# Attention scores in four 64x64 quarters of the array, two units at a time; probabilities times values in float32 without splits; the preceding block's values loaded from HBM

## The chip, the core and the metric

The program runs on one core of one Trainium2 chip. The metric is the device time of one execution in microseconds (us). Before the change the median of three runs is 838.9 us (837.33 to 839.96).

In the profile PE is TensorE multiplying, PEld is TensorE loading its stationary operand, DVE is VectorE, ACT is ScalarE, POOL is GpSimd, and SP is the engine that issues most transfers. L498 is line 498 of the kernel.

## The reference: what is computed

Attention with a window and a few global keys, then a mixture of experts:

```python
# q, k, v: [4 sequences, 8 heads, 768 tokens, 64]; n_global = 8, n_local = 96
scores = q @ k^T / 8 + bias[h, distance]          # bias: -slope(h) * distance
scores = where(global or 0 <= distance < n_local, scores, -1e9)
a = softmax(scores)
x = concat_heads(a @ v)                           # 3072 tokens x 512
logits = x @ w_gate + log1p(exp(x @ w_noise)) * noise
top 2 of 8 experts for each token, softmax over the two
out = sum over the two of  w * (relu(x @ w1[e]) @ w2[e])     # 512 -> 1024 -> 512
```

Everything is float32 in and out.

## The kernel before

The 3072 tokens are 24 blocks of 128, six to a sequence. A block of queries needs only its own 128 keys, the last 96 of the block before, and the 8 global keys. The 64 queries of one half of a block need 168 columns of keys in all (a window, `WIN`); in the first block of a sequence it is the block's own 128 columns.

**Units.** A unit is one block and one pair of heads; 24 blocks by 4 pairs make 96 units, and 16 of them belong to the first blocks of sequences. `score(n)` (from L488) makes the scores of unit n: for each half of the queries one float32 matmul, L498, with the queries of both heads as stationary operand. The query buffer holds the two heads of a pair on the two halves of the partitions, with zeros opposite (`clear`, L405), so that the contraction runs over all 128 rows and each head meets only its own keys. DVE then adds the bias and takes the extreme (L501), and ACT takes the exponential (L505). `trans(n)` (L510) turns the probabilities by TensorE (L519) and ACT writes them to SBUF as float16 (L521). `rest(n)` (L524) has DVE write what float16 lost, as a second float16 tile (L528). `attend(n)` (L533) multiplies by the values, L553: for each head and each of the two blocks of keys five 16-bit products, of two parts of the probabilities with three bfloat16 parts of the values. Each value row ends in a column of ones per head, so that the 65th output column is the softmax's denominator; every second unit DVE divides (L558 to L561).

**Values.** `load_v` brings a block's values from HBM. POOL splits them into the three parts (`split_v`, L356 and L357). `prev_v` copies the last 96 rows of the split tile to a tile of its own, from SBUF to SBUF (L363), and `keep_globals` does the same for the global keys' rows (L367).

**Order.** The program's order of instructions is the order written; no scheduler moves anything. In step n of the attention loop stand trans(n), score(n+2), rest(n), attend(n-2), and then what is due at that step: loads, the block's gate (`gate_t` L185, `gate_l` L193, `gate_s` L199), clearing of the output, weight loads and weight splits. Steps of the routing (`route`) are spread between as small DVE operations. `gate_l` runs in four 128x32 quarters of the array (a `tile_position` per matmul). SP issues transfers strictly in order and waits where a buffer is not free.

**Experts.** After the attention come eight experts, each with two matrices that are split into two float32r parts; their products (L737, L770, L780) fill TensorE. Expert 0's rows are gathered by table (`gather`, L147) and turned (`turn`, L164) at the attention's end.

**PSUM.** The eight banks are given out by tag: two for scores, two for turned probabilities, two for the products with values, one for the gate's temporaries, one for logits.

Of the kernel before, what the change touches and what calls it, by code (L numbers as in the profile page):

```python
# [10 lines left out]
F32 = mybir.dt.float32  # L11
FR = mybir.dt.float32r
F16 = mybir.dt.float16
# [17 lines left out]
def tile_local_global_attention_then_moe(  # L31
    ctx: ExitStack,
    tc: tile.TileContext,
    q: bass.AP,        # [B, 2, 2, D, S/128, H/2, 64]: halves of a sequence, then even and odd heads
    kT: bass.AP,       # [B, H*D, NB*(NG+P)]: each block of keys behind a copy of the first NG keys
    v: bass.AP,        # [B, NB, P, H*(D+1)]: a column of ones behind each head
    w_gn: bass.AP,     # [Dm, 2*E]: w_gate beside w_noise
    noise: bass.AP,    # [P, NT*E]
    w1: bass.AP,       # [E, Dm, F]
    w2: bass.AP,       # [E, F, Dm]  # L40
    n_global: int,
    n_local: int,
    out: bass.AP,      # [DUMP + N, Dm]
# [18 lines left out]
    SEG = [(0, 6), (6, 12), (12, 17), (17, 21), (21, NT)]   # blocks of tokens that are routed together  # L62
    CLOSE = 2        # after this part the first tiles of expert 0 are closed
# [11 lines left out]
    def bank(tag, bufs):  # L75
        return psum.tile([P, 512], F32, name=tag, tag=tag, bufs=bufs)
# [26 lines left out]
    # raw weights come in halves, in the order of their use  # L103
# [19 lines left out]
    def split(e, x, j, eng=nc.vector):  # L123
        """Piece j of 8 of a matrix into a part that the tensor engine takes as it is and the rest."""
# [29 lines left out]
    def spare_bank():  # L154
        spare[0] += 1
        return bank("m" if spare[0] % 2 else "lg", 1)
# [12 lines left out]
    NZ = 8      # pieces of the result that are cleared beside the attention  # L169
# [5 lines left out]
    # ---------------------------------------------------------------- gate  # L175
    XR, XT, LS = {}, {}, {}
    lg = bank("lg", 1)
    lgv = lg[:, :NT * 2 * E].rearrange("p (t e) -> p t e", t=NT)

    def gate_t(g):  # L180
        x = XR.pop(g).rearrange("p h d -> p (h d)")
        nc.sync.dma_start(xd[DUMP + g * P:DUMP + (g + 1) * P], x)
        ps = bank("m", 1).rearrange("p (k t) -> p k t", k=KC)
# [5 lines left out]
    def gate_l(g):  # L189
        ps = bank("m", 1)[:, :P]  # L190
# [13 lines left out]
    def route(r):  # L204
        """Routes a segment; a generator, to be resumed between steps of what runs beside it."""
# [97 lines left out]
        if r == CLOSE:  # L303
            # the first tiles of expert 0 are closed here: their products run while the rest is routed
# [10 lines left out]
    # ---------------------------------------------------------------- attention  # L315
    with ExitStack() as actx:
# [8 lines left out]
        def load_qk(b, j, i0):  # L325
            """Queries and keys of a block."""
# [615 lines left out]
```

## Time and profile before

| | |
|---|---|
| median of three runs | 838.9 us |
| span of the profiled execution, first to last instruction | 831.3 us |
| first matmul | 5.4 us after the span's start |
| attention, up to expert 0's first product | about 214 us |
| experts | about 617 us |
| PE busy over the span | 792.8 us, 95% |
| DVE, ACT, POOL busy | 379.5, 340.9, 278.4 us |
| mean granted clock of TensorE | 0.987 |

The profile does not record the profiled execution's own time, only its span; the median lies 7.6 us above that. Busy time on PE counts a matmul from its start until its modelled end, so a busy PE can still hold room between starts. How closely matmuls follow each other is read from the starts in the timeline. A float32 product appears as two rows for each instruction (L498: 192 instructions, 384 rows), a transpose as one.

### The profile page before, as it was taken

How to read it: one execution, taken by the hardware profiler on the slowest of the kernel's cores; microseconds unless marked ns; L12 is line 12 of the kernel's file. 1: busy time of each engine (PE TensorE's matmuls, PEld its weight loads, DVE VectorE, ACT ScalarE, POOL GpSimd, SP SyncE). 2: the span in 40 equal slices, each digit the busy share in tenths (PEclk: the TensorE clock that was granted, in tenths of full speed). 3: DMA queues.
4: the chain of work that ended last, by engine and by line, in shares of the span. 5: the costliest groups of instructions: out<-in, count | busy, mean ns of one | idle time of the engine just before them, and what ended most of it. 6: DMA issues, size and time to landing. Idle time of an engine off the chain costs nothing. (4 is left out here: it accounts for less than half of the span.)

```text
span 831.3 us, 16339 instructions
## 1 busy us (share of the span) xinstructions
PE 792.8 (95%) x6321; PEld 708.4 (85%) x6321; DVE 379.5 (46%) x1212; ACT 340.9 (41%) x736; POOL 278.4 (33%) x267
## 2 busy tenths in 40 slices
PE   5998999989898999999999999999999999999994
PEld 5987899878687989898989889898988889898983
DVE  7877889999640444233323332341333234233300
ACT  4766777666341343223323323332333333223311
POOL 8324565576455231314031321403141221212023
PEclk9998999999999999999999999999999999999998
DMA  8899979896456243435344534424344433432014
GB/s 193 229 302 260 261 204 265 222 223 160 175 103 123 66 130 113 96 76 142 102 62 122 131 76 97 118 75 109 114 92 114 105 80 116 96 77 30 1 25 61
DMA packets 86546, 106.93 MB, mean 129 GB/s; under 512 B 35563, under 2 KB 48107, under 8 KB 86459
## 3 DMA queue, kind: packets, MB, share of 16 engines
q1 hardware_dynamic: 71194, 79.10, 34.0%
q0 software_dynamic: 15264, 26.69, 17.4%
q8 instruction: 52, 0.85, 0.4%
q14 instruction: 36, 0.29, 0.1%
HBM read 67.20 MB, written 28.24 MB: 115 GB/s over the span
## 5 line engine op out<-in xcount | busy, mean ns | idle before, releaser
L755 POOL DMA_INDIRECT out_dram<-y,tba x28 | 44.4, 1587 | 257.7 <-ACT y L754 257.7
L132 DVE TENSOR_TENSOR w1l<-raw,w1h 128x512 fp32r<-128x512 f32 x56 | 38.3, 690 | 148.0 <-ACT w1h L131 148.0
L770 PE MATMUL av<-w2h,hh 128*128 128x512 f32 x256 | 102.8, 401 | 0.0
L770 PE MATMUL av<-w2h,hl 128*128 128x512 f32 x256 | 101.3, 396 | 0.0
L770 PE MATMUL av<-w2l,hh 128*128 128x512 f32 x256 | 101.1, 395 | 0.0
L505 ACT ACTIVATE a<-ns,mx 128x168 f32<-128x168 f32 (+1 forms) x192 | 72.6, 423 | 54.7 <-DVE mx L501 46.9
L737 PE MATMUL at<-xh,w1h 128*128 128x512 f32 (+1 forms) x256 | 90.1, 352 | 0.0
L737 PE MATMUL sc<-xh,w1h 128*128 128x512 f32 (+1 forms) x256 | 89.6, 350 | 0.0
L737 PE MATMUL at<-xl,w1h 128*128 128x512 f32 (+1 forms) x256 | 89.2, 349 | 0.2 <-DVE xl L167 0.2
L737 PE MATMUL at<-xh,w1l 128*128 128x512 f32 (+1 forms) x256 | 89.2, 349 | 0.0
L737 PE MATMUL sc<-xh,w1l 128*128 128x512 f32 (+1 forms) x256 | 88.6, 346 | 0.0
L737 PE MATMUL sc<-xl,w1h 128*128 128x512 f32 (+1 forms) x256 | 88.5, 346 | 0.0
L755 POOL DMA_INDIRECT out_dram<-y,tbb x24 | 38.2, 1592 | 147.5 <-ACT y L754 147.2
L748 DVE SCALAR_TENSOR_TENSOR hl<-sc,hh 128x300 fp32r<-128x300 f32 (+1 forms) x62 | 35.8, 578 | 103.7 <-ACT hh L747 103.7
L780 PE MATMUL av<-hh,w2h 128*128 128x300 f32 x256 | 78.9, 308 | 0.0
L780 PE MATMUL av<-hl,w2h 128*128 128x300 f32 x256 | 76.9, 300 | 0.0
L780 PE MATMUL av<-hh,w2l 128*128 128x300 f32 x256 | 76.9, 300 | 0.0
L498 PE MATMUL sc<-ks,qbuf 128*128 128x168 f32 (+1 forms) x384 | 71.6, 312 | 5.4 <-DMA qbuf<-in_q 5.4
L747 ACT ACTIVATE hh<-sc 128x300 fp32r<-128x300 f32 (+1 forms) x62 | 31.5, 508 | 100.2 <-PE sc L737 100.2
L553 PEld LDWEIGHTS <-ah 128*128 128x128 f16 (+1 forms) x1056 | 63.5, 98 | 9.9 <-DMA vp<-vs 4.2
L754 ACT ACTIVATE y<-av,tba 128x512 f32<-128x512 f32 x28 | 19.3, 689 | 126.0 <-issue 106.2
L747 ACT ACTIVATE hh<-at 128x300 fp32r<-128x300 f32 (+1 forms) x62 | 31.5, 508 | 86.8 <-PE at L737 86.8
(149 smaller groups left out, 1877.6 us busy)
## 6 DMA issues: line engine op xcount, KB each, us to landing
raw<-in_w SPq DMA_DIRECT2D x32, 1024.0 KB
vp<-vs SPq DMA_DIRECT2D x20, 487.5 KB
out_dram<-zero SPq DMA_DIRECT2D x14, 512.0 KB
vs<-in_v SPq DMA_DIRECT2D x24, 260.0 KB
qbuf<-in_q SPq DMA_DIRECT2D x48, 128.0 KB
xd<-xr SPq DMA_DIRECT2D x24, 256.0 KB
ks<-in_k SPq DMA_DIRECT2D x20, 272.0 KB
ks<-in_k SPq DMA_DIRECT2D x4, 464.0 KB
```

The lines of the kernel that those rows point to most:

```text
L132: eng.tensor_sub(lo, t, hi.bitcast(F32))
L498: nc.tensor.matmul(ps[:, s], qs[b, j][:, 2 * i0 + s, hp], ks[b, j][:, hp, k0:k0 + w], start=True, stop=True)
L505: nc.scalar.activation(A[n][:, s, c:c + w], ns[:, s, :w], AF.Exp, bias=mx[:, s:s + 1], scale=-1.0)
L553: nc.tensor.matmul(ps[:, h % 4], x, y, start=j == 0, stop=j == len(todo) - 1)
L737: nc.tensor.matmul(ps, w[:, k, fs], x[c][:, k], start=n == 0, stop=n == 3 * KC - 1)
L747: nc.scalar.activation(hh[c][:, f], ps, AF.Relu)
L748: nc.vector.scalar_tensor_tensor(hl[c][:, f], ps, 0.0, hh[c][:, f].bitcast(F32), op0=OP.max, op1=OP.subtract)
L754: nc.scalar.activation(y, ps, AF.Copy, scale=r[:, 1:2].bitcast(F32))
L755: ins = nc.gpsimd.indirect_dma_start(out=out, out_offset=bass.IndirectOffsetOnAxis(ap=r[:, 0:1], axis=0), in_=y, in_offset=None, bounds_ch ...
L770: nc.tensor.matmul(ps, x[0][:, f, cols], w[:, f], start=n == 0, stop=n == 3 * FC - 1)
L780: nc.tensor.matmul(ps, w[:, f, cols], x[1][:, f], start=n == 0, stop=n == 3 * FC - 1)
```

## The change

Three things, and what they bring along:

- **Scores.** `product(n)` makes the scores of units n and n+1 together. The two heads of a unit now lie on the same partitions of the query buffer and those of its neighbour on the other half, without zeros; so each of eight matmuls has 64 rows of contraction, 64 columns of stationary operand and 168 (or 128) moving columns, at one of four positions of the array. Unit n writes one PSUM bank and unit n+1 another. `score(n)` keeps only the DVE and ACT part. The clearing of the query buffers is gone, and queries come in one transfer for each block instead of two.
- **Values.** Turned probabilities are written as one float32 tile, `rest` is gone, and `attend` makes one float32 product where five 16-bit ones stood. `split_v` is gone.
- **Preceding values.** `load_v` also loads the preceding block's last 96 rows, and in the first blocks of a sequence the global rows, from HBM into one of four tiles.

PSUM banks are now given out in rings: three for scores, two shared by turned probabilities and the gate's temporaries, two for products with values, one for logits; from the experts on it is two, two and one as before. Comments are dropped and heads are paired differently (a unit's heads are 4u'+x and 4u'+x+2), which changes no amount of work.

```diff
+    rings = {"sc": [0, 1, 2], "at": [3, 4], "m": [3, 4], "av": [5, 6], "lg": [7]}
...
-            for x in range(2):
-                nc.sync.dma_start(qs[b, j][x * D:(x + 1) * D, n, :, x].rearrange("p n k t -> p (n k) t"),
-                                  q[b, j, x, :, n].rearrange("p n k t -> p (n k) t"))
+            nc.sync.dma_start(qs[b, j][:, n].rearrange("p n k t -> p (n k t)"),
+                              q[b, j].rearrange("x d n k t -> (x d) n k t")[:, n].rearrange("p n k t -> p (n k t)"))
...
         def load_v(g):
             b, i = divmod(g, NB)
-            t = aw.tile([P, 2 * HD + HD // 2], F32, name="vs", bufs=4)
-            vs[g] = t
-            nc.sync.dma_start(t[:, :HD], v[b, i])
...
-            nc.gpsimd.tensor_sub(t[:, HD:2 * HD], t[:, :HD], p1)
-            nc.gpsimd.tensor_sub(p3, t[:, HD:2 * HD], p2)
...
+            vs[g] = aw.tile([P, HD], F32, name="vs", bufs=4)
+            nc.sync.dma_start(vs[g], v[b, i])
             if i:
-                vp[g] = vpb[i % 2]
-                nc.sync.dma_start(vp[g][:NP], vs[g - 1][P - NP:])
...
+                vp[g] = vpb[g % 4]
+                nc.sync.dma_start(vp[g][:NP], v[b, i - 1, P - NP:])
+                if i <= 4:
+                    nc.sync.dma_start(vp[g][NP:], v[b, 0, :NG])
...
+        def product(n):
+            g, u, b, i = geo(n)
+            w = WIN if i else P
+            j, i0 = divmod(i, NBH)
+            for x in range(2):
+                SC[n + x] = bank("sc")[:, :2 * w].rearrange("p (s w) -> p s w", s=2)
+            for s in range(2):
+                k0 = i0 * KB + s * Q if i else NP + NG
+                for y in range(2):
+                    for x in range(2):
+                        r = slice(x * D, (x + 1) * D)
+                        nc.tensor.matmul(SC[n + x][y * Q:(y + 1) * Q, s], qs[b, j][r, 2 * i0 + s, u + y],
+                                         ks[b, j][r, u + y, k0:k0 + w], start=True, stop=True,
+                                         tile_position=(x * D, y * Q))
...
-                nc.tensor.matmul(ps[:, s], qs[b, j][:, 2 * i0 + s, hp], ks[b, j][:, hp, k0:k0 + w],
-                                 start=True, stop=True)
...
-            hi = aw.tile([P, 512], F16, name="ah", bufs=4)
-            nc.scalar.activation(hi[:, :2 * w], ps, AF.Copy, scale=UP)
-            AT[n] = hi, ps
-
-        def rest(n):
-            hi, ps = AT[n]
-            w = ps.shape[1] // 2
-            lo = aw.tile([P, 512], F16, name="al", bufs=4)
-            nc.vector.scalar_tensor_tensor(lo[:, :2 * w], ps, UP, hi[:, :2 * w], op0=OP.mult, op1=OP.subtract)
-            AT[n] = hi, lo
+            AT[n] = aw.tile([P, 512], F32, name="at", bufs=4)[:, :2 * w]
+            nc.scalar.activation(AT[n], ps, AF.Copy)
...
-                    p1, p2, p3 = parts(t)
-                    cc = slice(s * w + c0, s * w + c0 + P)
-                    todo += [(hi[:kk, cc], p1[:kk, c]), (hi[:kk, cc], p2[:kk, c]), (hi[:kk, cc], p3[:kk, c]),
-                             (lo[:kk, cc], p1[:kk, c]), (lo[:kk, cc], p2[:kk, c])]
...
+                    nc.tensor.matmul(ps[:, h % 4], a[:kk, y * w + c0:y * w + c0 + P], t[:kk, c],
+                                     start=kk < P or not i, stop=kk == P)
...
+            product(0)
             score(0)
             score(1)
+            product(2)
             for n in range(NPAIR + LAG):
                 if n < NPAIR:
                     trans(n)
                 if n + 2 < NPAIR:
                     score(n + 2)
-                if n < NPAIR:
-                    rest(n)
...
                     attend(n - LAG)
+                if n % 2 and n + 3 < NPAIR:
+                    product(n + 3)
                 tick()
```

How TensorE's order changes, between one block's `gate_l` and its `gate_s`, in the middle of the attention. In the rows `at` is the turned probabilities in PSUM (L519), or after the change also their SBUF copy (L533), `ah` and `al` are its two 16-bit parts, `sc` the scores, `av` the products with values, `vs` and `vp` the values of the block and of the one before. Before, one step of the loop, for a unit with both blocks of keys (the ten loads and products of the unit's other head, which read the same, are left out):

```order
L193 MATMUL m<-xt,wgn 32x128 x4
L519 MATMUL at<-ident,a_180 128x2x64 x4
L498 MATMUL sc<-ks,qbuf_105 128x168 x2
L553 LDWEIGHTS ah
L553 MATMUL av<-vp_102,ah 128x65
...
L553 LDWEIGHTS al
L553 MATMUL av<-vp_102,al 128x65
...
L199 MATMUL lg<-sel,ls 128x16
```

After the change, two steps, up to the next `gate_l`:

```order
L206 MATMUL lg<-sel,ls 128x16
L513 MATMUL at<-ident,a_180 128x2x64 x4
L533 MATMUL av<-vp_103,at 128x65
L533 MATMUL av<-vs,at 128x65
...
L485 MATMUL sc<-ks,qbuf_107 64x168 x8
L513 MATMUL at<-ident,a_181 128x2x64 x4
L533 MATMUL av<-vp_104,at 128x65
...
L485 MATMUL sc<-ks,qbuf_107 64x168 x8
L200 MATMUL m<-xt,wgn 32x128 x4
```

The two score matmuls that stood in every step between the transposes and the products with values now stand as one group of eight in every second step, behind the products; every second such group is followed at once by the gate's four 128x32 matmuls. Twenty loads and twenty products of a unit become four products that bring their own load.

DVE's order over two units, before:

```order
L528 SCALAR_TENSOR_TENSOR al<-at,ah 128x512
L501 ISA ns,mx<-sc,bias 128x168
L501 ISA mx 128x1
...
L528 SCALAR_TENSOR_TENSOR al<-at,ah 128x512
L558 TENSOR_SCALAR den<-av 128x4
L559 RECIPROCAL den<-den 128x4
L561 TENSOR_TENSOR xr<-av,den 128x256
```

and after:

```order
L497 ISA ns,mx<-sc,bias 128x168
L497 ISA mx 128x1
...
L539 TENSOR_SCALAR den<-av 128x4
L540 RECIPROCAL den<-den 128x4
L542 TENSOR_TENSOR xr<-av,den 128x256
```

One 128x512 operation for each unit is gone; the rest keeps its order.

SP's queue over one block, before:

```order
L363 DMA vp_103<-vs 96x1300
L182 DMA xd<-xr 128x512
L345 DMA vs<-in_v 128x520
L332 DMA ks<-in_k 128x4x136
L336 DMA qbuf_104<-in_q 64x8x64 x2
```

and after:

```order
L189 DMA xd<-xr 128x512
L351 DMA vs<-in_v 128x520
L354 DMA vp_102<-in_v 96x520
L356 DMA vp_102<-in_v 8x520
L339 DMA ks<-in_k 128x4x232
L342 DMA qbuf_107<-in_q 128x512
```

The rows of the preceding block now follow the load of the block's own values, three blocks ahead of their use and without POOL between, where they stood one block ahead behind POOL's split.

More of the change, by code (lines that the diff above doesn't have):

```diff
@@ L73, in tile_local_global_attention_then_moe, with bank @@
     gp = wctx.enter_context(tc.tile_pool(name="gp", bufs=1))
-    def bank(tag, bufs):
-        return psum.tile([P, 512], F32, name=tag, tag=tag, bufs=bufs)
+    rings = {"sc": [0, 1, 2], "at": [3, 4], "m": [3, 4], "av": [5, 6], "lg": [7]}
+    turns = {}
+    def bank(tag):
+        ring = rings[tag]
+        key = tuple(ring)
+        turns[key] = turns.get(key, -1) + 1
+        return psum.tile([P, 512], F32, name=tag, tag=f"b{ring[turns[key] % len(ring)]}", bufs=1)
     xd = dram.tile([N + DUMP, Dm], F32, name="xd")
@@ L155, in spare_bank @@
         spare[0] += 1
-        return bank("m" if spare[0] % 2 else "lg", 1)
+        return bank("m" if spare[0] % 2 else "lg")
     def turn(e, t, ps=None):
@@ L189, in gate_l @@
     def gate_l(g):
-        ps = bank("m", 1)[:, :P]
+        ps = bank("m")[:, :P]
         x = XT.pop(g)
@@ L401, in biases @@
                 for h in heads:
-                    x = h % 2
-                    nc.vector.tensor_scalar(to[x * Q:(x + 1) * Q, h // 2], d, -slopes[h] / scale, None, op0=OP.mult)
-            def clear(e, j, n):
-                for x in range(2):
-                    e.memset(qbuf[j][(1 - x) * D:(2 - x) * D, n, :, x], 0.0)
+                    u, y = h // 4 * 2 + h % 2, h // 2 % 2
+                    nc.vector.tensor_scalar(to[y * Q:(y + 1) * Q, u], d, -slopes[h] / scale, None, op0=OP.mult)
             t = small.tile([P, 1], F32, name="t")
@@ L496, in score @@
             for s in range(2):
-                k0 = i0 * KB + s * Q if i else NP + NG
-                nc.tensor.matmul(ps[:, s], qs[b, j][:, 2 * i0 + s, hp], ks[b, j][:, hp, k0:k0 + w],
-                                 start=True, stop=True)
-            for s in range(2):
                 nc.vector.tensor_tensor_reduce(
-                    out=ns[:, s, :w], in0=ps[:, s], in1=bias[:, hp, s] if i else bias0[:, hp, s],
+                    out=ns[:, s, :w], in0=ps[:, s], in1=bias[:, u, s] if i else bias0[:, u, s],
                     scale=-scale, scalar=3e38, op0=OP.add, op1=OP.min, accum_out=mx[:, s:s + 1])
@@ L542, in attend @@
                 blocks.insert(0, (vp[g], NP + NG, 0))
-            for s in range(2):
-                h = 2 * hp + s
+            for y in range(2):
+                h = u // 2 * 4 + 2 * y + u % 2
                 c = slice(h * D1, (h + 1) * D1)
-                todo = []
                 for t, kk, c0 in blocks:
-                    p1, p2, p3 = parts(t)
-                    cc = slice(s * w + c0, s * w + c0 + P)
-                    todo += [(hi[:kk, cc], p1[:kk, c]), (hi[:kk, cc], p2[:kk, c]), (hi[:kk, cc], p3[:kk, c]),
-                             (lo[:kk, cc], p1[:kk, c]), (lo[:kk, cc], p2[:kk, c])]
-                for j, (x, y) in enumerate(todo):
-                    nc.tensor.matmul(ps[:, h % 4], x, y, start=j == 0, stop=j == len(todo) - 1)
-            if hp % 2:
-                if hp == 1:
+                    nc.tensor.matmul(ps[:, h % 4], a[:kk, y * w + c0:y * w + c0 + P], t[:kk, c],
+                                     start=kk < P or not i, stop=kk == P)
+            if u % 2:
+                if u == 1:
                     XR[g] = gp.tile([P, H, D], F32, name="xr", bufs=2)
                 den = aw.tile([P, 4], F32, name="den", bufs=2)
-                nc.vector.tensor_scalar(den, ps[:, :, D], UP * 1e-9, None, op0=OP.add)
+                nc.vector.tensor_scalar(den, ps[:, :, D], 1e-9, None, op0=OP.add)
                 nc.vector.reciprocal(den, den)
-                h0 = 2 * hp - 2
+                h0 = 2 * u - 2
                 nc.vector.tensor_mul(XR[g][:, h0:h0 + 4], ps[:, :, :D],
@@ L731, in up @@
         def up(e, c, f, spared=False, between={}):
-            ps = bank("sc" if f % 2 else "at", 2)[:, :hh[c].shape[2]]
+            ps = bank("sc" if f % 2 else "at")[:, :hh[c].shape[2]]
             fs = slice(f * P, (f + 1) * P)
@@ L816, in tile_local_global_attention_then_moe @@
         for t in range(TB):
-            turn(0, TA + t, bank("sc", 2) if t == TB - 1 else None)
+            turn(0, TA + t, bank("sc") if t == TB - 1 else None)
         for t in range(3):
```

81 lines of the change are left out of this document (29 added, 52 removed).

## The prediction

> **What bounds the kernel now.** I read the page's span, then a table of stretches, then what PE waited for, then PE's timeline. The stretches were cut where PE's busy time changes; columns are busy time (and instructions) of PE, PEld, DVE, ACT, POOL, then granted clock, DMA share and GB/s:
>
> ```profile
> span 831.3 us, 16339 instructions
> ...
> 0.00:5.40 5.40, 0.00 (x0) 0.03 (x1) 3.35 (x11) 1.49 (x2) 4.05 (x21) 1.00 0.57 142
> 5.40:20.00 14.60, 11.37 (x83) 10.38 (x84) 11.63 (x44) 6.16 (x18) 12.63 (x23) 0.91 0.96 219
> 20.00:45.00 25.00, 24.72 (x391) 23.01 (x388) 20.20 (x92) 18.80 (x46) 8.28 (x13) 0.98 0.86 227
> 45.00:48.00 3.00, 1.30 (x19) 1.09 (x18) 2.28 (x9) 1.83 (x5) 0.00 (x0) 1.00 1.10 321
> 48.00:76.00 28.00, 27.91 (x446) 26.08 (x443) 21.54 (x102) 21.18 (x55) 10.94 (x10) 1.00 1.06 288
> 76.00:84.00 8.00, 4.09 (x38) 3.84 (x37) 4.15 (x15) 3.25 (x9) 2.81 (x3) 0.68 1.12 259
> 84.00:101.00 17.00, 16.20 (x247) 14.78 (x247) 14.63 (x73) 12.11 (x30) 9.27 (x9) 0.95 1.03 262
> 101.00:157.00 56.00, 56.00 (x929) 52.73 (x929) 51.32 (x258) 41.91 (x108) 28.62 (x28) 1.00 0.87 224
> 157.00:183.00 26.00, 21.69 (x329) 19.62 (x328) 24.63 (x125) 15.19 (x42) 18.78 (x19) 1.00 0.96 225
> 183.00:203.00 20.00, 20.00 (x330) 18.71 (x327) 17.15 (x79) 14.27 (x36) 11.95 (x14) 1.00 0.72 199
> 203.00:214.00 11.00, 8.20 (x146) 6.99 (x142) 9.07 (x45) 6.17 (x14) 3.90 (x4) 1.00 0.52 168
> 214.00:831.00 617.00, 601.28 (x3399) 531.20 (x3398) 199.51 (x369) 198.52 (x380) 167.20 (x128) 0.99 0.39 93
> ```
>
> The change touches the first 214 us. For long runs there (101 to 157, 183 to 203) PE has no idle time: the stage goes at PE's pace. Idle time of PE is 5.4 us until the first matmul, 3.2 in 5.4 to 20, and 13.9 after that: 1.7 at 45, 3.9 at 76, 0.8 in 84 to 101, 4.3 in 157 to 183, 2.8 in 203 to 214, 0.4 elsewhere. What ended PE's waits before 214 us (total, times, longest):
>
> ```profile
> PE av L553 <- DMA vp<-vs: 5.6, 2, 3.9
> PE sc L498 <- DMA qbuf<-in_q: 5.4, 1, 5.4
> PE at L519 <- DVE al L528: 3.3, 3, 1.7
> PE m L185 <- DVE xr L561: 3.2, 5, 1.4
> PE lg L199 <- ACT ls L196: 1.5, 1, 1.5
> PE sc L164 <- DMA xg<-xd,tb: 0.9, 1, 0.9
> ```
>
> So the copy of the preceding values costs 5.6 us in two stalls, and most of the rest waits for DVE, which was busy 24.63 of the 26 us from 157 to 183. So two things decide: what the change does to PE's work, and which stalls go.
>
> **PE's work, part by part.** PE's timeline in an undisturbed stretch (start, duration of the group, count):
>
> ```profile
> 130.67 0.60 PE L519 MATMUL at<-ident,a 128*128 128x128 f32 x4
> 131.10 0.74 PE L498 MATMUL sc<-ks,qbuf 128*128 128x168 f32 x4
> 131.68 0.26 PE L553 MATMUL av<-vp,ah 104*128 104x65 bf16 x3
> ...
> 132.25 0.23 PE L553 MATMUL av<-vs,al 128*128 128x65 bf16 x2
> 132.41 0.43 PE L193 MATMUL m<-xt,wgn 128*32 128x128 f32 x8
> 132.76 0.66 PE L519 MATMUL at<-ident,a 128*128 128x128 f32 x4
> 133.26 0.74 PE L498 MATMUL sc<-ks,qbuf 128*128 128x168 f32 x4
> ...
> 134.46 0.37 PE L199 MATMUL lg<-sel,ls 128*128 128x16 f32 x2
> 134.68 0.64 PE L519 MATMUL at<-ident,a 128*128 128x128 f32 x4
> ```
>
> From start to start: four transposes take 0.43 us (0.108 each); four score rows 0.58 (0.145 each); the twenty 16-bit products of a unit about 0.64 (131.68 to 132.32), 0.032 each. The number of units of each kind:
>
> ```profile
> L498 PE MATMUL sc<-ks,qbuf 128*128 128x168 f32 x320 | 60.1, 311 | 0.0
> L498 PE MATMUL sc<-ks,qbuf 128*128 128x128 f32 x64 | 11.5, 314 | 5.4 <-DMA qbuf<-in_q 5.4
> ```
>
> Four rows a unit: 80 full units and 16 of first blocks.
>
> *Values in float32.* A full unit has four products of two rows each, with a new 128x128 float32 stationary operand at every row and 65 moving columns. The trace has this operand with 16 moving columns (L199: two rows in 134.68 - 134.46 = 0.22 us, 0.11 each) and, in the transposes, with 128 (0.108). Both sides of 65 columns give 0.108, so I take 0.108: 8 x 0.108 = 0.86 against 0.64, **+0.22 us** for 80 units (+17.9), and 4 x 0.108 against 10 x 0.032, +0.11, for 16 (+1.8). Sum **+19.7**: fewer instructions, more time. Streaming alone would be 65/168 x 0.145 = 0.056 a row, a gain; L199 speaks against that, since 16 columns took no less than 128.
>
> *Scores in quarters.* Two full units cost 8 x 0.145 = 1.16 us before. After, eight small matmuls of two rows stand in four quarters; if four run at once they take four rounds of 0.145, 0.58. Whether quarters run at once is seen on L193: eight rows of 128 columns, four side by side, in 132.41 to 132.76, where one after another they would need 8 x 0.108 = 0.86. They do. But leaving and entering the mode isn't free: from the end of the products (132.32) L193 takes until 132.76, and the transposes behind it take 0.50, 0.07 more than at 130.67: 0.51 us for two rounds of 0.108, so 0.29 for a round trip. Then a product costs 0.58 + 0.29 = 0.87, -0.29 x 40; with 128 columns, at 0.145 x 128/168 = 0.11 a row, 4 x 0.11 + 0.29 = 0.73 against 0.88, -0.15 x 8. Sum **-12.8**. Every second product has L193 right behind it, from one such mode to the next: one of four passages falls away, 0.145 x 22 = **-3.2**. No trace here shows a split by rows; below it is four rounds free of passages (-0.58 x 40 - 0.44 x 8 = -26.7), above it eight rounds with them (1.45 against 1.16, 1.17 against 0.88: +13.9).
>
> The Trainium skill weighs this otherwise: "TensorE: Matmul & The Clock Gate", Part 3, gives four tiles a measured 3.07-fold. By it two full units would cost 16 x 0.145 / 3.07 = 0.76 and the scores would gain about 6 us more than by L193 (0.11 x 40 + 0.16 x 8). Here each pack stands between full-array work, as L193 does, so I stay with that row.
>
> PE's work in all: 19.7 - 12.8 - 3.2 = **+3.7 us**, or +0.15 for a block of about 7.8 (four units of 0.43 + 0.58 + 0.64, and the gate's 0.43 + 0.51 + 0.22). On PE alone this change is a small loss.
>
> **What stalls go.** *The preceding values.* They came one block ahead, behind a load, a split on POOL and SP's queue. Now they come from HBM three blocks ahead (some 24 us), and SP waits only for a buffer that the block before has just left. Both stalls go: -5.6. And after the long one PE ran with a low clock (0.68 in 76 to 84):
>
> ```profile
> 80.84 0.35 PE L553 MATMUL av<-vp,ah 104*128 104x65 bf16 x3 [3.91 <-DMA vp<-vs]
> ...
> 81.94 1.10 PE L185 MATMUL m<-ident,xr 128*128 128x128 f32 x4
> 82.82 1.06 PE L519 MATMUL at<-ident,a 128*128 128x128 f32 x4
> 83.68 1.33 PE L498 MATMUL sc<-ks,qbuf 128*128 128x168 f32 x4
> 84.80 0.37 PE L553 MATMUL av<-vp,ah 104*128 104x65 bf16 x3
> ```
>
> Twenty products took 1.10 for 0.64, four transposes 0.88 and 0.86 for 0.43, four score rows 1.12 for 0.58: 1.9 us lost. Together **-7.5**. What hides the loads: DMA carries less than before.
>
> ```profile
> vp<-vs SPq DMA_DIRECT2D x20, 487.5 KB
> qbuf<-in_q SPq DMA_DIRECT2D x48, 128.0 KB
> ```
>
> 487.5 KB become 195 (520 of 1300 columns by the shapes), and queries come in half as many transfers with runs of 2 KB instead of 256 bytes. If that cover fails, up to 5.6 come back.
>
> *DVE.* These go:
>
> ```profile
> L528 DVE SCALAR_TENSOR_TENSOR al<-at,ah 128x512 f16<-128x512 f32 x80 | 54.6, 683 | 2.0 <-ACT ah L521 2.0
> L356 POOL TENSOR_TENSOR vs<-vs 128x520 f32<-128x520 f32 x24 | 25.6, 1068 | 53.6 <-DMA vs<-in_v 42.0 <-PE m L185 9.6 <-PE av L553 2.0
> ```
>
> 0.68 us a unit is 19 of DVE's 51.3 us in 101 to 157 (28 units at 7.8 us for four). There PE is the bound and this is worth nothing; from 84 to 101 and 157 to 183, where routing steps crowd DVE, it is worth most of 0.8 + 4.3: **-4.0**. Nothing is late next: ACT does the same copies and exponentials, 41.9 of 56 us.
>
> *Start.* PE's waits from 5.5 to 24 us hold
>
> ```profile
> PE at L519 <- DVE al L528: 2.4, 2, 1.7
> ```
>
> of 3.2 us idle, and that operation is gone; queries need one transfer, not two, and no clearing. Between 0 and 5 (all 3.2 and a third of the first load's 5.4); I take **-3.0**.
>
> *End.* Of the 2.8 us in 203 to 214, the gathered rows of expert 0 end 0.9; their chain of transfers keeps its length while PE comes sooner, so what DVE gives back the gather takes: **-0.3**.
>
> *New waits.* The scores of two units now come in a burst every second step, and the turned probabilities share two banks with the gate. Bounds 0 and 3; I take **+1.5**. The experts, 617 us, run as before.
>
> **Sum.** 3.7 - 7.5 - 4.0 - 3.0 - 0.3 + 1.5 = **-9.6 us**: the profiled span of 831.3 becomes 821.7. The median is 7.6 above the span, and I carry that over: 838.9 - 9.6 = **829.3 us**.
>
> **The rivals.**
>
> 1. *The quarters don't all run at once.* The two row halves take turns: eight rounds, +13.9 instead of -12.8, so 829.3 + 26.7 = **856, slower**. For it: nothing here shows a split by rows. Against: L193's four columns overlap fully. It turns the sign from about 5.4 rounds a product (9.6 us over 48 products is 0.20, 1.4 rounds). A rule of the Trainium skill leads this way too ("TensorE: Matmul & The Clock Gate", Part 3: matmuls start and end strictly in program order). The mechanism here would be that the second row of one matmul holds up the next quarter: nine rounds, 34 us above the forecast, 863; L193's eight rows in 0.43 speak against that order.
> 2. *Passages between modes overlap with other work.* Then 0.29 goes 48 times, less the 3.2 already counted: -10.7, **819**. For it: loads of stationary operands run ahead elsewhere. Against: L193 shows the gap every time.
> 3. *Stalls by DVE stay*, because the chain through routing and gather sets the pace from 157 on, and the start is bound by latency: only -7.5 + 3.7 is left, **835**.
> 4. *A burst of scores starves PE*: transposes wait for the exponentials once in every product. At 0.5 us each, 24 us, **853, slower**. Against: between a product and its first transposes lie two steps, about 4 us at this pace, and ACT was busy 1.5 us a unit (41.91 us for 28).
>
> **Chances.** Forecast 0.62, rival 1 0.10, rival 2 0.08, rival 3 0.10, rival 4 0.07, anything else 0.03. Faster by over 0.3% (2.5 us, about what a measurement here can tell from no change): 0.57 + 0.08 + 0.07 = 0.72; within 0.07; slower 0.21, rivals 1, 4 and the tails. The forecast's own range is 821 to 837; 8 in 10 lie in 817 to 848, with rival 2 below, rival 3 inside, and rivals 1 and 4 above it only in part.
>
> **What would show it.** Right: L485 groups of eight that hold PE about 0.87 us and rows four abreast; L533 rows 0.108 apart; a block at 7.9 to 8.0 us against 7.8; no PE wait on `vp`; DVE at about 60% in the middle of the attention; expert 0's first product near 204 us (214 less 9.6). Wrong: L485 over 1.2 us; L533 rows off 0.1; PE waits on L501 or L505 in every second step; first expert product not before 212.

## The result, and the profile after

| | before | after |
|---|---|---|
| median, runs side by side | 838.1 us (837.3 to 840.0, 4 runs) | **813.1 us** (810.8 to 815.7, 4 runs) |
| ratio | | **0.971** (0.969 to 0.974) |
| profiled span | 831.3 us | 812.6 us |
| first gate matmul `gate_l` | 25.08 us | 19.09 us |
| expert 0's first product | 213.6 us | 195.8 us |
| from there to the end | 617.7 us | 616.8 us |

25 us faster. The forecast was 829.3 us with a range of 817 to 848: the sign was right, the size was not. The changed kernel's profiled execution took 814.3 us, 1.7 more than its span. Medians in this document are over all executions of a kernel in a set, and ratios leave out those that took over 1.5% longer than the kernel's fastest.

The table of stretches of the changed kernel, cut where its own busy time changes (columns as before: busy time and instructions of PE, PEld, DVE, ACT, POOL, then granted clock, DMA share, GB/s), and below it all that PE waited for before 197 us:

```profile
span 812.6 us, 14768 instructions
...
0.00:4.80 4.80, 0.04 (x4) 0.07 (x5) 2.15 (x9) 1.49 (x2) 3.55 (x17) 1.00 0.57 171
4.80:15.00 10.20, 9.88 (x112) 7.91 (x112) 7.34 (x45) 6.63 (x20) 1.99 (x16) 1.00 1.05 315
15.00:40.00 25.00, 25.00 (x300) 22.36 (x293) 13.51 (x83) 18.41 (x46) 1.97 (x7) 1.00 0.80 247
40.00:90.00 50.00, 49.96 (x624) 44.47 (x623) 29.81 (x189) 40.48 (x104) 10.18 (x8) 1.00 0.85 272
90.00:140.00 50.00, 50.00 (x623) 45.01 (x623) 29.75 (x202) 36.99 (x96) 11.98 (x12) 1.00 0.75 188
140.00:160.00 20.00, 20.00 (x266) 17.60 (x266) 15.79 (x113) 15.12 (x42) 11.80 (x13) 1.00 0.80 184
160.00:179.00 19.00, 19.00 (x233) 16.88 (x232) 10.38 (x65) 14.26 (x36) 9.73 (x10) 1.00 0.98 237
179.00:196.00 17.00, 13.94 (x115) 13.25 (x112) 7.83 (x44) 7.29 (x16) 4.66 (x5) 0.78 0.34 110
```
```profile
PE sc L485 <- DMA qbuf<-in_q: 4.8, 1, 4.8
PE sc L171 <- DMA xg<-xd,tb: 3.1, 1, 3.1
PE sc L485 <- DVE mx L497: 0.3, 1, 0.3
```

From 15 to 179 us PE has next to no idle time (0.04 us) and a clock of 1.00. The waits for `vp`, `al` and `xr` are gone. DVE, nearly full from 157 to 183 us before (24.63 of 26 us), is now busy 60% of the time in the middle (29.75 of 50 us). One wait is new in size: the gather of expert 0's rows.

PE's timeline of the changed kernel in the middle of the attention (start, duration of the group, count):

```profile
114.86 0.60 PE L513 MATMUL at<-ident,a 128*128 128x128 f32 x4
115.30 0.34 PE L533 MATMUL av<-vp,at 104*128 104x65 f32 x2
...
116.23 0.80 PE L485 MATMUL sc<-ks,qbuf 64*64 64x168 f32 x16
116.96 0.43 PE L200 MATMUL m<-xt,wgn 128*32 128x128 f32 x8
117.32 0.66 PE L513 MATMUL at<-ident,a 128*128 128x128 f32 x4
...
118.85 0.64 PE L513 MATMUL at<-ident,a 128*128 128x128 f32 x4
119.32 0.34 PE L533 MATMUL av<-vp,at 104*128 104x65 f32 x2
119.49 0.39 PE L533 MATMUL av<-vs,at 128*128 128x65 f32 x2
119.71 0.39 PE L533 MATMUL av<-vp,at 104*128 104x65 f32 x2
119.94 0.39 PE L533 MATMUL av<-vs,at 128*128 128x65 f32 x2
120.25 0.80 PE L485 MATMUL sc<-ks,qbuf 64*64 64x168 f32 x16
120.99 0.66 PE L513 MATMUL at<-ident,a 128*128 128x128 f32 x4
121.48 0.33 PE L533 MATMUL av<-vp,at 104*128 104x65 f32 x2
```

Sixteen score rows hold PE from 120.25 to 120.99, 0.74 us. Around them lie the two passages: the eight rows of values ahead take 0.93 instead of 8 x 0.108 = 0.86, and the transposes behind take 0.49 instead of the 0.44 of 114.86 to 115.30. 0.74 + 0.07 + 0.05 = **0.86 us** for a product with its passages. The quarters do run four at once.

**Where the 18.7 us between the spans lie.** I measure blocks, from one `gate_l` to the next; 22 of them lie ahead of expert 0. An undisturbed full block was 7.86 us and is 7.90; the blocks around a sequence's first have less work and are shorter.

| part | us |
|---|---|
| start, up to the first `gate_l` | -6.0 |
| PE's work in undisturbed blocks, 22 x 0.05 | +1.1 |
| the two blocks that waited for `vp` (9.71 and 14.41 for 7.86) | -8.4 |
| all other stalls in blocks (what is left over) | -9.9 |
| the gather's wait, in the last block before expert 0 | +3.1 |
| last `gate_l` before expert 0 to its first product, 4.87 to 7.17 | +2.3 |
| experts | -0.9 |

Of the 9.9 us of other stalls, the profile of before shows 6.9 as idle time of PE: 5.0 us of it end with DVE, 1.9 with ACT. The rest shows as no idle time.

The other 6 us of the 25 are no part of the change's work. They are the difference between executions: the shown execution of before was about 5 us faster than that kernel's median, that of after 1.2 slower.

### The profile page after: what moved, and what is told of

It reads as the page before. It is cut to its first block, busy times and chain, and to the rows that moved or that the text cites. A ratio compares the mean times of both kernels' runs of the same rounds, so it can differ in the third digit from the quotient of the medians.

```text
span 812.6 us, 14768 instructions
## 1 busy us (share of the span) xinstructions
PE 789.2 (97%) x5649; PEld 698.8 (86%) x5649; DVE 316.2 (39%) x1114; ACT 338.9 (42%) x736; POOL 223.6 (28%) x215
## 5 line engine op out<-in xcount | busy, mean ns | idle before, releaser
L533 PE MATMUL av<-vs,at 128*128 128x65 f32 x384 | 72.1, 277 | 0.0
L304 POOL DMA_INDIRECT tbl<-ent,sli x48 | 48.1, 1002 | 65.4 <-DVE mx L497 41.4
```

Of the source, the lines that this page charges most:

```text
L304: ins = nc.gpsimd.indirect_dma_start(out=tbl, out_offset=bass.IndirectOffsetOnAxis(ap=sli[:, i, j:j + 1], axis=0), in_=ent[:, i, j], in_of ...
L533: nc.tensor.matmul(ps[:, h % 4], a[:kk, y * w + c0:y * w + c0 + P], t[:kk, c], start=kk < P or not i, stop=kk == P)
```

## The experiments

A set is one group of kernels run side by side, with runs of the kernel before among them. Ratios are against those, with 95% intervals. Where a set's kernel before took 835 to 836 us (838 above), it compares with the result above. The last three sets are another matter and stand apart below.

### Which part brings it

**Scores alone.** The changed kernel, its new order of PSUM banks included, with the values' path as it was before:

```diff
+            nc.gpsimd.tensor_sub(t[:, HD:2 * HD], t[:, :HD], p1)
+            nc.gpsimd.tensor_sub(p3, t[:, HD:2 * HD], p2)
...
+                nc.sync.dma_start(vp[g][:NP], vs[g - 1][P - NP:])
...
+            nc.vector.scalar_tensor_tensor(lo[:, :2 * w], ps, UP, hi[:, :2 * w], op0=OP.mult, op1=OP.subtract)
```

> The changed kernel with the values, their split and the SBUF copy as before the change; only the scores in quarters (with their query loads and PSUM rings) are new. TensorE's work for a block falls from 7.86 to about 7.05 us, but DVE still does the remainder operation and was busy 51.3 of 56 us. Theory A (the gain of the whole change is stalls and start, not TensorE work): DVE cannot follow, blocks stay at 7.4 us or more and the stalls on vp and DVE stay or grow: time 828 to 838. Rival B (the cheaper scores are what made the kernel faster): blocks near 7.1 us, about 16 us gained: 818 to 823.

**Values alone.** The kernel before, with float32 values and no splits; scores and the copy of the preceding values within SBUF as before:

```diff
+                    nc.tensor.matmul(ps[:, h % 4], a[:kk, s * w + c0:s * w + c0 + P], t[:kk, c],
+                                     start=kk < P or not i, stop=kk == P)
...
-                    at(n + 1, split_v, g + 2)
...
-                    rest(n)
```

> The kernel before with only the values part: one float32 probability tile, float32 products, no remainder on DVE, no split on POOL; scores with 128 rows and zeros, and the preceding values copied from SBUF, as before. TensorE's work for a block rises from 7.86 to about 8.65 us. Theory A: +16 us of TensorE work, against it the DVE stalls (6.6 us), part of the start (3) and part of the vp stall (0 to 8.6): 838 to 848, not faster. Rival B (DVE and POOL held the kernel, TensorE's work does not count): 818 to 826.

**Values alone, preceding values from HBM**, as in the change:

```diff
-                nc.sync.dma_start(vp[g][:NP], vs[g - 1][P - NP:])
+                nc.sync.dma_start(vp[g][:NP], v[b, i - 1, P - NP:])
```

> As the values-only kernel, with the preceding values loaded from HBM three blocks ahead. If the copy from SBUF still stalls TensorE once the split is gone, this is faster than the values-only kernel by up to 8.6 us; if the stall came from POOL's split ahead of the copy, the two are equal within 2 us. Theory A expects equal.

**The change without HBM:** the changed kernel with the copy within SBUF, one block ahead as before; the same two lines the other way round.

> The changed kernel with the preceding values copied from the block's tile in SBUF one block ahead, as before the change, instead of loaded from HBM. Theory A (the stall came from the split on POOL ahead of the copy): 812 to 815, as the changed kernel. Rival (the load from HBM itself took the stall away): 819 to 823, with PE waits on vp of 5 us or more.

Measured: scores alone 837.4 us (ratio 1.002, 0.999 to 1.005); values alone 827.8 (0.990, 0.987 to 0.993); values alone from HBM 828.2 (0.990, 0.986 to 0.995); the change with the SBUF copy 813.3 (0.972, 0.967 to 0.977). So alone the scores bring nothing, the values 8 us, and both together 25. The values alone came out between the two accounts, of which one expected no gain and the other 818 to 826 us. Loading the preceding values from HBM brings nothing that these runs can tell (their intervals are 2 to 4 us to either side). One of the five executions of the change with the SBUF copy took 2716 us, with blocks of 25.61 us for 7.90 at a recorded clock of 1.00; no run shows why, and as it is the profiled one, no trace shows that kernel at its usual time.

The waits show why the scores alone are worth nothing. PE's waits up to 216 us in the kernel with scores alone, and one of its stretches:

```profile
PE at L533 <- DVE al L542: 20.5, 25, 1.9
...
PE m L192 <- DVE xr L575: 3.2, 8, 0.7
PE av L567 <- DMA vp<-vs: 2.0, 1, 2.0
```
```profile
155.00:185.00 30.00, 23.05 (x426) 18.66 (x424) 27.23 (x142) 18.43 (x48) 19.52 (x20) 1.00 0.82 214
```

TensorE's shorter work turned into 20.5 us of waiting for DVE's second half of the split (`al`), 25 times: the transposes need the PSUM bank that this operation still reads. The kernel with scores alone also has the change's PSUM banks, where the transposes share two with the gate; how much of the waiting comes from that, no run parts. With values alone nothing of the kind is left up to 216 us:

```profile
PE sc L484 <- DMA qbuf<-in_q: 6.0, 1, 6.0
PE sc L164 <- DMA xg<-xd,tb: 2.1, 1, 2.1
PE m L185 <- DVE xr L532: 0.4, 1, 0.4
```

Its undisturbed blocks are 8.58 us and regular, against 7.86: TensorE works 0.72 us longer in each full block, about 15 in all (0.3 to 0.8 in those around a sequence's first), and still the kernel is 8 us faster. About 23 us of stalls had to go for that, by this estimate. On top of it the scores save 8.58 - 7.90 = 0.68 us a full block, 14.0 over the 21 blocks ahead of the gather's wait, and now nothing stops them.

### Which engine's relief it was

**The kernel before, once more**, for how much one execution differs from the next.

> The kernel before, profiled once more. Its profiled execution had a span of 831.3 us, about 833 of time, where its timed runs lie between 832.7 and 842.7. Theory: executions differ by how long TensorE waits for the copied values (5.6 us in the first profile) and for the clock after that; a slower execution should show waits on vp above 5.6 us, its blocks without a stall again at 7.86 us. Rival: executions differ in the experts or everywhere, with vp waits again near 5.6.

It took 837.1 us with a span of 835.2, so 1.9 us lie around a span. Its undisturbed blocks are the same (7.86), its stalls are not. The third block takes 12.40 us where it took 9.71, the seventh 9.21 where it took 14.41, and the waits are:

```profile
PE av L553 <- DMA vp<-vs: 6.4, 4, 2.8
...
PE at L519 <- DVE al L528: 3.8, 4, 1.7
PE m L185 <- DVE xr L561: 3.7, 5, 1.4
PE sc L164 <- DMA xg<-xd,tb: 2.3, 1, 2.3
```

**One DVE operation put back** into the changed kernel, unused, of the size of the removed one, reading the same PSUM bank:

```diff
+                    nc.vector.scalar_tensor_tensor(lo[:, :w], ps, 32768.0, AT[n], op0=OP.mult, op1=OP.subtract)
```

> The changed kernel with one VectorE operation of the old remainder's size and source put back for each unit, its result unused. TensorE's work stays at 7.9 us a block. Theory (VectorE with that operation is the bound wherever routing runs): blocks without routing stay near 7.9 us, those with routing go to 9 to 10.5 us as in the scores-only kernel, in all 10 to 16 us more: 823 to 829. Rival (it was POOL's split and its hold on VectorE that mattered): 813 to 817.

Measured 835.4 us (0.9997, 0.995 to 1.004): this kernel has lost the whole gain, more than either account allowed. The row of the operation and PE's wait:

```profile
L676 DVE SCALAR_TENSOR_TENSOR al<-at 128x512 f16<-128x512 f32 (+1 forms) x96 | 61.9, 645 | 43.0 <-ACT at L515 42.5
```
```profile
PE at L513 <- DVE al L676: 9.6, 17, 1.3
```

An undisturbed block becomes 8.31 us, +0.41, of which 0.19 show as idle time of PE; over 22 blocks that is 9 us. The rest is stalls and low granted clock. The time of its executions goes with their mean clock: 828.5 us at 0.996, 840.6 at 0.977. The first of these, beside the changed kernel's 810.8 us at 0.995, makes the operation 17.6 us where the clock holds; what the median has above that goes with a lower clock. The order of PSUM banks is the changed kernel's, so this isn't what the operation cost in the kernel before.

**The two POOL operations put back**, unused:

```diff
+            nc.gpsimd.tensor_sub(x[:, :HD], t, t)
+            nc.gpsimd.tensor_sub(x[:, HD:].bitcast(BF), x[:, :HD], t)
```

> The changed kernel with POOL's two operations of the old split put back for each block, on the same tiles at the same places, their results unused. Theory (POOL off the path, VectorE no longer near its limit): 812 to 816. Rival (POOL holds VectorE up while it runs, or its waits delay the routing's table): 818 or more.

Measured 822.2 us (0.983, 0.975 to 0.990): 9 us of the 25 come back, and the account that priced POOL's split at nothing falls. The blocks are those of the changed kernel, except two late ones that take 4.8 us more, and the gather's wait is gone; but the first `gate_l` comes at 27.2 us instead of 19.1. From 7 to 19 us DVE's rows read in this kernel, and below in the changed one:

```profile
L398 DVE TENSOR_SCALAR bias<-dist 64x336 f32<-64x336 f32 x8 | 8.2, 1059 | 0.0
```
```profile
L392 DVE TENSOR_SCALAR bias<-dist 64x336 f32<-64x336 f32 x8 | 2.3, 323 | 0.0
```

The operation that makes the biases takes 1.06 us instead of 0.32 while POOL's subtractions (1.05 to 1.29 us each) run; before it took 0.75. PE then waits 1.9 us for DVE and goes on at a granted clock of 0.50 in 20 to 24 us. The Trainium skill has a rule that fits ("SBUF — State Buffer", "SBUF: two separate sides": a VectorE operation in a two-port mode and a GpSimd operation take their shared port pair exclusively, and the one that comes second blocks for the whole instruction of the other). The trace agrees in size: the added 0.74 us is within one POOL operation. That the bias operation ran in such a mode, no run shows.

**Values alone, with a second transfer** that brings the bytes of the copy back to those before:

```diff
+                nc.sync.dma_start(big[i % 2], bias0.rearrange("p k s w -> p (k s w)")[P - NP:, :HD + HD // 2])
```

> The values-only kernel, with each copy of preceding values followed by a second transfer of 96 x 780 columns within SBUF, so that the bytes are those of the old copy (487.5 KB). Theory (the old stalls came from the transfers' load: the copy stood in SP's queue while the DMA engines were full): waits on vp come back for some executions, 830 to 838 against 827.8. Rival (the stalls came from POOL's split before the copy): 826 to 830 and no waits on vp.

Measured 827.3 us (0.993, 0.989 to 0.996), blocks of 8.58 and no wait on `vp`. So a copy within SBUF, with as many bytes moved as before, brings no `vp` stalls back. What is left of the removed things is that the copy had to wait for POOL's split; that is by elimination, and no run puts that order back alone.

### The same kernels where the gain was lost

The next set gave 861.7 us for the kernel before, and the two sets after it 862.1 and 862.9. The expectations call this the third chip, on which it was first seen; the last set ran on the chip numbered as that of the second set, where the kernel before had taken 835.6. What differs there the runs don't tell.

**The changed kernel again**, with two variants: the turning of expert 0's rows moved behind the attention's last products, so that the gather has work over it, and besides that a shorter routing segment.

```diff
-                if n >= NPAIR - 1:
-                    t = n - NPAIR + 1
-                    turn(0, t, bank("sc"))
...
+            for t in range(TA):
+                turn(0, t, bank("sc"))
```

> The changed kernel as it is, beside the next two on the same chip: 811 to 815, with the wait of some 3 us for expert 0's gathered rows at the attention's end.

> The changed kernel with the four turns of expert 0's rows moved behind the last products with values, so that TensorE does the remaining attention while the gathers land. About 2.5 us of work stands ahead of the first turn then. Theory (the 3.1 us wait for gathered rows and the low clock behind it cost 3 to 5 us): 808 to 811. Rival (the chain of gathers sets expert 0's start whatever stands ahead, and the turns now pile up behind one another): 812 to 815.

> As the late turns, and with the routing segment that closes expert 0's first tiles four blocks long instead of five (the one before takes seven). Its chain has eight table writes instead of ten on POOL, at 1.28 us each, so the gathers land 2.6 us earlier. Theory: the wait for gathered rows falls to nothing: 806 to 810. Rival: as the late turns alone.

Measured 861.1, 861.2 and 859.0 us, ratios 0.997 (0.994 to 1.000), 0.997 (0.993 to 1.000), 0.998 (0.994 to 1.001): no gain that counts, for any of them. The variants can't be judged there, since the changed kernel itself has no gather wait in that set: its attention ends some 50 us later and the rows are there. The 811 to 815 us expected for it were missed by 46.

**Four kernels side by side**, to part a low clock from delays and to time the DVE operation again:

> The kernel before, for its trace beside the three others. Two accounts of the third chip, on which the changed kernel took as long as the kernel before (861.14 against 861.65 us): (clock) TensorE was granted less there whenever it had been busy without a break for some 80 us, and the changed kernel, which has no breaks, loses more to that than the kernel before. Then the kernel before keeps undisturbed blocks of 7.86 us on any chip, and on a chip with a low clock it shows stretches of 0.5 to 0.8 granted clock of its own, fewer than the changed kernel; on a chip without, 831 to 838 us with stalls on the preceding values and VectorE. (delay) The third chip delayed signals between engines or transfers; then its stalls are on transfers at a full clock.

> The changed kernel once more. Where the granted clock stays at 1.00 up to the last 20 us of attention: 811 to 816 us, blocks of 7.9 us, ratio 0.97. (clock) If the chip grants 0.5 to 0.8 in stretches of attention, each stretch of 18 us costs 8 to 10 us, with no engine ahead of TensorE late, and the ratio goes to 0.98 to 1.00. (delay) If the ratio is near 1 at a full clock, the loss is in waits on transfers.

> The changed kernel with the turning of expert 0's rows moved behind attention's last products, so that the gather of those rows (waited for 3.1 us in the changed kernel) has TensorE work over it. Theory: the wait at L171 on xg goes, 810 to 812 us where the changed kernel takes 813, ratio to it 0.996 to 0.998. Rival: the 3 us come back as a wait of expert 0's first product for the turned rows or their split, 813 us, no difference.

> The changed kernel with an unused VectorE operation per unit, of the size of the split's second half, once more. Its first runs gave back the whole gain (835 us), but its profiled execution had stretches of 0.50 to 0.70 granted clock. By its undisturbed blocks (8.31 against 7.90 us) it costs 0.41 us x 23 = 9.4 us: (clock) 820 to 824 us where the clock holds. (VectorE) 828 to 836 us if VectorE's turn itself makes stalls beyond that at full clock.

Measured: before 861.5, the changed kernel 858.3 (0.993, 0.989 to 0.997), late turn 861.9 (0.999, 0.995 to 1.002), DVE operation back 872.6 (1.012, 1.007 to 1.017). Up to 96 us the changed kernel runs as ever: blocks of 7.90, no idle time, clock 1.00. Stretches of it around that point:

```profile
80.00:96.00 16.00, 16.00 (x214) 14.42 (x213) 8.68 (x65) 12.57 (x32) 3.83 (x3) 1.00 0.56 170
96.00:112.00 16.00, 10.38 (x125) 8.57 (x125) 4.53 (x32) 7.37 (x21) 10.01 (x10) 0.89 0.76 207
112.00:128.00 16.00, 12.14 (x107) 10.74 (x105) 7.00 (x42) 7.53 (x20) 1.96 (x3) 0.68 0.28 83
128.00:156.00 28.00, 28.00 (x354) 25.30 (x353) 16.57 (x119) 19.93 (x50) 0.00 (x0) 1.00 0.52 163
```

PE halts first and the clock falls after it, while POOL is busy: PE's first break of over 1 us starts at 103.4 us, and the clock is 1.00 until 108 us, 0.66 from 108 to 110 and 0.50 from there to 122. What POOL does there is a burst of twelve indirect writes of the routing table (L304). The second burst, with the waits of the first 15 us of it above and rows of its timeline below:

```profile
ACT at L515 <- remote: 8.9, 1, 8.9
...
PE at L513 <- issue: 7.0, 1, 7.0
DVE ns L497 <- remote: 4.1, 2, 3.9
```
```profile
162.46 0.44 PE L192 MATMUL m<-ident,xr 128*128 128x128 f32 x2 [0.48 <-DVE xr L542]
163.16 0.98 POOL L304 DMA_INDIRECT tbl<-ent,sli  x1 [0.30 <-issue]
164.45 0.98 POOL L304 DMA_INDIRECT tbl<-ent,sli  x1 [0.31 <-issue]
...
169.48 0.38 ACT L515 ACTIVATE at<-at 128x256 f32<-128x256 f32 x1 [8.88 <-remote]
169.58 0.98 POOL L304 DMA_INDIRECT tbl<-ent,sli  x1 [0.30 <-issue]
...
169.91 0.69 PE L513 MATMUL at<-ident,a 128*128 128x128 f32 x2 [7.01 <-issue]
```

PE stands still for 7.0 us, ACT for 8.9 and DVE for 3.9, while POOL writes every 1.28 us. The profile names no cause: "issue" is a wait for nothing that it shows, "remote" a signal that it puts down to no instruction or transfer of the program. From 15 to 208 us all breaks of PE over 2 us in this kernel begin in its three bursts (twelve, twelve and ten writes); in the changed kernel's first profile the same writes make none (above, 90 to 160 us). So the account by the clock falls, as TensorE halts at a full clock. For the account by delayed transfers or signals nothing speaks but these unnamed waits; it stays open.

**Twice the writes**, the second time into a table that nothing reads, and **the first burst spaced** by idle work on POOL, beside the late turn without spacing:

```diff
+                ins = nc.gpsimd.indirect_dma_start(
+                    out=tbl2, out_offset=bass.IndirectOffsetOnAxis(ap=sli[:, i, j:j + 1], axis=0),
```
```diff
+                if r == 0:
+                    for _ in range(4):
+                        nc.gpsimd.memset(idle_s, 0.0)
```

> The changed kernel with each of GpSimd's 48 indirect writes of the routing table (L304, 1.28 us from one to the next) issued a second time, into a table that nothing reads. On the third chip all breaks of over 2 us in TensorE's work fell into the bursts of these writes (7.9, 10.2 and 7.1 us idle in three bursts, and a clock of 0.6 to 0.7 there and after), on the others none did. (writes) If the writes hold up the other engines on that chip, twice the writes make twice the breaks there: 880 to 900 us against 858. (else) On a chip where the bursts make no breaks, or if they only coincide: the routing that closes before expert 0 comes some 15 us later on GpSimd, its gather waits, 815 to 835 us there, 858 to 875 on the third chip.

> The changed kernel with the turning of expert 0's rows behind attention's last products. On a chip where the clock holds, 810 to 812 us if the gather's 3.1 us are the cost, 813 if they come back. On the third chip 858 to 862 as before.

> The same with the first burst's 12 table writes spaced apart by idle memsets on GpSimd (2.5 us from one to the next in place of 1.28; the kernel before had 1.9 there, from its splits between them, and lost 7 us in that burst on the third chip where the changed kernel lost 11). (writes) On the third chip the two blocks of the first burst fall from 11.5 and 15.2 us toward 8 to 10, and the time by 5 to 8 us; if the loss is per write and not by their density, no change. On a chip where the bursts cost nothing: no change from the late turn alone, 810 to 814 us.

Measured: writes doubled 916.2 us (1.063, 1.059 to 1.066); late turn 862.2 over four executions (855.2, 855.6, 868.8 and 868.9); late turn with the first burst spaced **846.7** (0.980, 0.975 to 0.984). Doubling cost even more than the 880 to 900 us expected. Spacing one burst of three won 8.7 us against the late turn's two quicker executions, where 5 to 8 were expected; with so few of them that difference is rough. The spaced writes came 2.8 us apart, not 2.5:

```profile
102.14 1.02 POOL L304 DMA_INDIRECT tbl<-ent,sli  x1 [0.49 <-issue]
...
104.98 0.98 POOL L304 DMA_INDIRECT tbl<-ent,sli  x1 [0.45 <-issue]
```

The burst's stretch, without spacing and with it:

```profile
96.00:112.00 16.00, 9.58 (x90) 7.84 (x86) 3.39 (x23) 4.75 (x14) 11.97 (x12) 0.72 0.58 157
112.00:128.00 16.00, 13.88 (x116) 12.65 (x120) 6.75 (x42) 8.61 (x22) 0.00 (x0) 0.64 0.27 82
```
```profile
96.00:112.00 16.00, 16.00 (x207) 13.94 (x206) 10.35 (x63) 12.82 (x35) 10.33 (x23) 1.00 0.84 239
112.00:128.00 16.00, 16.00 (x191) 14.37 (x191) 10.05 (x71) 11.54 (x29) 12.34 (x29) 1.00 0.86 218
```

The two blocks of that burst fall from 12.90 and 15.73 us to 6.14 and 7.00, 15.5 us less, which are the changed kernel's undisturbed lengths. The profiled spans differ by 3.8 us only (853.5 and 849.7), so most of that is lost again later. The other two bursts, left at 1.28 us, still stop PE there, by up to 7.1 us. That is shown, then: close-packed table writes stop the core under this condition, at 2.8 us apart the first burst does not, and the low clock is what follows. Not shown is why the same writes stop nothing in the first sets, nor by what path they stop the other engines.

It also says why the gain was lost there. In the kernel before, POOL's splits stand between the writes: its first burst took 23 us where the changed kernel's takes 15. Set against the first profiled executions, the blocks with bursts cost the kernel before about 30 us more, the changed kernel about 46 (13.6, 18.4 and 13.9 in its three bursts). Without the splits the writes come closer together, and by this comparison the change pays for it.

The second run of the DVE operation agrees with its first. In the ten blocks ahead of the first burst it makes 86.3 us out of 76.8: +4.1 by 0.41 a block and +5.4 in stalls and low clock (0.91 from 60 to 80 us, which is worth 1.8). At that rate 22 blocks cost 21 us, 17 without the low clock. The first run had 22 us by the medians and 17.6 where the clock held. The kernel before took 85.0 to 86.0 us for these blocks in its two undisturbed profiles.

## Why the prediction was right or wrong

Of the forecast's own signs of being right all but one came true: expert 0's first product came at 195.8 us, not near 204. The terms of the sum, one by one:

- **Scores in quarters, -12.8 and -3.2: right.** 0.86 us a product against 0.87; on top of the values they save 14.0 us in 21 of 24 blocks, against 16.0 forecast for all. The rivals fall: the quarters don't take turns (rival 1), the passages stay (rival 2), the exponentials starve nothing (rival 4; the only wait is 0.3 us). The Trainium skill has 3.07-fold for four tiles, measured with 32 rows and 512 columns each ("TensorE: Matmul & The Clock Gate", Part 3). Here the pack by itself is 16 x 0.145 / 0.74 = 3.1-fold, and 2.7-fold with the passages around it, which the forecast was right to count. The Trainium skill's rule of strict order (the same part), by which nine rounds were to be feared, made no ninth round: the transposes start 0.74 us after the scores.
- **Values in float32, +19.7: too much.** About 15 by the blocks, 0.18 us a unit and not 0.22. PE's work came out at +1.1 instead of +3.7.
- **Preceding values, -7.5: right in size, wrong in cause.** 8.4 us went in two blocks. But the step, though it named POOL's split among what the copy stood behind, credited the load from HBM, three blocks ahead; two runs show no gain from this part, and the stalls go with the splits, by elimination.
- **DVE, -4.0: this is the step that failed.** It read "there PE is the bound and this is worth nothing" from a stretch with no idle PE, and counted only idle time where DVE was crowded. By the two profiled spans the stalls other than those on `vp` went by 9.9, most of them DVE's. In the changed kernel, putting the operation back costs about 18 us where the clock holds and 22 by the medians: it stands in the chain from the transposes to the free PSUM bank, it adds 0.41 us to every full block there, and with it in place TensorE's savings become waits (20.5 us with scores alone). So the overlap was wrong: cheaper TensorE work and the DVE operation can't be priced one by one. How much of this comes from the new order of PSUM banks stays open. Rival 3, by which DVE's stalls would stay, fell.
- **Start, -3.0: half of it, and without its main cause.** 6.0. The forecast looked at the DVE operation and the queries' transfers, not at POOL's first splits beside DVE's biases: put back into the changed kernel, they cost 8.1 us there.
- **End, -0.3: wrong sign.** +5.4, as 3.1 for the gather and 2.3 at a low clock behind it. The text had the mechanism ("what DVE gives back the gather takes") but gave it the 0.3 us of one small difference, though PE was to come 9.6 us sooner and the gather's chain was to keep its length. New waits, +1.5, didn't come.
- **The 7.6 us between span and median: a wrong assumption.** Only 1.7 to 1.9 us lie around a span. The rest was an execution with few stalls, about 5 us better than the median, so the stalls that could go were larger than the one profile showed. This carry-over is the sum's largest single error: it alone hid 6 of the 15 us that were missing.

Signed, the errors of the sum add up: PE -2.6, `vp` -0.9, DVE -5.9, start -3.0, end +5.7, new waits -1.5, experts -0.9, profile against median -6.3: together -15.4, which is what lies between -9.6 and -25.0.

## What to carry to other kernels

Before pricing an operation on a second engine at nothing because TensorE is busy, follow what waits for its result or its buffer: put the one operation back, or take it away, and time that. Two edits can be worth nothing and 8 us alone and 25 together, when the first only lengthens the waits that the second removes. Compare the profiled execution's own time, not its span, with the median, before taking one profile's stalls for the kernel's; and a burst of indirect writes from GpSimd is worth pacing where engines stop without a named cause. Here that made a version of 846.7 us, against 862.9 for the kernel before and 855.4 for the late turn without pacing in the same set; it was not run beside the changed kernel itself, nor under the first condition, nor with all bursts spaced.

## What was not expected of the hardware

- A VectorE operation of 0.32 us took 1.06 us beside GpSimd subtractions that nothing in it depends on.
- While POOL made ten or twelve indirect table writes 1.28 us apart, TensorE stopped for up to 7.1 us at a stretch in the changed kernel, and ScalarE and VectorE stopped too, in three sets of runs; in the others the same writes made no such stop. With the first burst 2.8 us apart, TensorE did not stop in it.
- In the first burst's stops of the changed kernel TensorE's granted clock fell to 0.50 and stayed there for some 12 us, so a stall costs more than its idle time: 9.5 us idle (96 to 128 us) made the two blocks 13.6 us longer.
